# The last 96 columns of gate and up with rows on partitions, turned by a DMA transpose

## The chip, the cores and the metric

The kernel runs on one core of a Trainium2 chip. Its engines are TensorE (PE, which multiplies matrices and whose weight loads the profile lists as PEld), VectorE (DVE), ScalarE (ACT), GpSimd (POOL) and SyncE (SP, which issues DMA transfers). The metric is the device time of one execution in microseconds, as the median of several runs.

## What is computed

One transformer block on 2048 rows of 512 columns, in bf16. The first half is attention with 32 heads of 16 columns over a window of 8 rows, two apart; the second is a gated feed-forward layer of width F = 1376. `_ln` is the layernorm without weights:

```
h  = x + attention(_ln(x) @ wqkv) @ wo
n  = _ln(h)
gate = n @ W_gate                  # 512 x 1376
up   = n @ W_up                    # 512 x 1376
out  = h + (relu(gate) * up) @ W_down   # 1376 x 512
```

The feed-forward width is 1376 = 10 x 128 + 96. The 96 columns left over, the tail, are what the change is about.

## The kernel before

The rows are cut into four chunks of 512 (`tk` 0 to 3). For each chunk the kernel makes the layernorm, turns the result so that the 512 columns stand on partitions (four blocks `dt` of 128), forms q, k and v, makes the attention, projects with wo (L831) and adds the residual, makes the second layernorm into `hnT` (again columns on partitions, 128 x 4 x 512), and runs the feed-forward layer.

Gate and up are formed with the feature on partitions. For each block `ft` of 128 features, four matmuls (one per `dt`) have 128 x 128 of the weights as the stationary operand and 512 rows of `hnT` as the moving one (L869); one group of four makes up, one makes gate, each in a PSUM bank of its own. ACT copies up out of its bank (L873) and takes the relu of gate out of the other (L876); DVE multiplies two blocks at a time (L897) into `gT`, which has features on partitions and so can be the stationary operand of the down matmuls (L914) as it is. The eleventh block is the tail: the same 8 matmuls of 512 columns, but with 96 weight columns, and evictions and a product of 96 x 512. The down matmuls make, for each 128 rows, 11 matmuls of 512 columns into a bank; they come as a first part of blocks 0 to 7 and a second part of blocks 8 to 10, the tail among these. DVE adds the residual (L925) and a DMA stores the rows. In the last chunk the last 128 rows are done in two halves of 256 columns.

All of this is written as a list of steps, each with an engine, a planned duration, what it depends on and which buffers it takes. A planner (`Plan.order`) turns the list into one order for each engine. The rank of every step stands in a table of numbers, `RANK`, and on each engine steps go by rank, so that steps of different chunks are interleaved: gate and up of one chunk run on PE while DVE is still busy with the next chunk's attention. The engines carry out their streams strictly in this order. Buffers are taken from small sets: eight PSUM banks for everything, two each for `up_sb` and `gr`, seven for `gT`, five for rows of 128 x 512 (`row`, which serves normalised rows, squares and output rows).

Transfers: SP issues the loads at the start, the broadcasts of the attention weights (`big<-ex`, L730), the stores, and ten DMA transposes of normalised rows (L505) in its own order, one after the other; POOL issues the transfers that add halves of the attention products (L805). The other normalised rows are turned on PE by matmuls with the identity (L516).

Of the kernel before, what the change touches and what calls it, by code (L numbers as in the profile page):

```python
# [8 lines left out]
P = 128  # L9
BF16 = mybir.dt.bfloat16  # L10
# [81 lines left out]
class Plan:  # L92
# [9 lines left out]
    def add(self, key, *a, **k):  # L102
        op = Op(*a, **k)
        op.key = key
        op.seq = len(self.ops)
        if RANK:
            op.prio = RANK[op.seq]
        self.ops.append(op)
        for b in set(op.take) | set(op.use):
            b.left += 1  # L110
        return op
# [97 lines left out]
def kernel(  # L209
# [63 lines left out]
    wg_sb = sb.tile([P, NT, F], BF16, name="wg_sb")  # L273
    wu_sb = sb.tile([P, NT, F], BF16, name="wu_sb")
# [31 lines left out]
    def setup():  # L306
# [27 lines left out]
        nc.sync.dma_start(wu_sb[:], B_W_up.rearrange("(dt p) f -> p dt f", p=P))  # L334
        nc.sync.dma_start(wg_sb[:], B_W_gate.rearrange("(dt p) f -> p dt f", p=P))
# [45 lines left out]
    HSP = ()  # L381

# [157 lines left out]
    for tk in range(NCK):  # L540
# [317 lines left out]
        for f0 in range(0, NFT, 2):  # L858
            fts = range(f0, min(f0 + 2, NFT))
            ub, gr, gt = Buf(up_s), Buf(gr_s), Buf(gT_s)  # L860
            eds = []
            for ft in fts:
# [4 lines left out]
                def f_mm(w_sb, mm, lo=0, hi=CS, ft=ft, fs=fs, hnT=hnT):  # L867
                    for dt in range(NT):
                        nc.tensor.matmul(mm.t[:fs, lo:hi], lhsT=w_sb[:, dt, ft * P: ft * P + fs],  # L869
                                         rhs=hnT.t[:, dt, lo:hi], start=(dt == 0), stop=(dt == NT - 1))  # L870
# [7 lines left out]
                def mm(w_sb, b, wl, pr=pr, f0=f0, ft=ft, f=f_mm, hnT=hnT):  # L878
                    if (tk, ft) not in HSP:
                        return add(("mm%d" % (f0 // 2), tk), "PE", 4 * MM, lambda: f(w_sb, b), hev + [wload[wl]], pr,  # L880
                                   take=[b], use=[hnT], lat=PEL)
                    a = None
                    for i, (lo, hi, evs) in enumerate(((0, 2 * P, hev[0:1]), (2 * P, CS, hev[1:]))):
                        a = add(("mm%d%s" % (f0 // 2, "ac"[i]), tk), "PE", 2 * MM + 0.005, lambda lo=lo, hi=hi: f(w_sb, b, lo, hi),
                                evs + [wload[wl], a], pr, take=[b], use=[hnT], lat=PEL if i else 0.0)
                    return a

                a = mm(wu_sb, um, "u")
                b = add(("ue%d" % (f0 // 2), tk), "ACT", A5, f_ue, [a], pr - 200, take=[ub], use=[um], lat=AL)
                c = mm(wg_sb, gm, "g")  # L890
# [14 lines left out]
        if tk == NCK - 1:  # L905
            parts[-1:] = [(BPC - 1, 0, D // 2), (BPC - 1, D // 2, D)]
# [77 lines left out]
```

## Time and profile before

| | |
|---|---|
| median of 3 runs | 199.99 us (199.97 to 200.69) |
| the profiled execution | 201.04 us |
| its span, from the first to the last instruction | 199.3 us |
| PE busy | 193.6 us, 1099 matmuls |
| DVE busy | 153.2 us |
| ACT busy | 114.2 us |
| tail matmuls (128x96 weights, 512 columns) | 32 records of 379 ns |
| first to last matmul of the feed-forward layer | 66.93 to about 196.1 us |

An engine's busy time is the sum of the time in which it had an instruction in work. Matmuls are pipelined: one record of 512 columns has 379 ns, but the next begins about 216 ns after it, so their records overlap. In the lines below, "x16" is the number of instructions, "128x512" the partitions and elements of the tile written, and a bracket or the last column tells for how long the engine sat idle before and what ended that time.

### The profile page before, as it was taken

The page shows a single profiled execution, that of the slowest core. Times are in us where ns is not written, and L with a number is a line of the kernel's source. Part 1 is how long each engine was busy: PE and PEld are TensorE (multiplying, and loading weights), DVE is VectorE, ACT ScalarE, POOL GpSimd, SP SyncE. Part 2 cuts the span into 40 slices and gives each one's busy share as a digit, 9 for nine tenths or more (in the row PEclk, how much of TensorE's full clock was granted, in tenths as well). Part 3 has the DMA queues.
Part 4 walks back from the last instruction along what each step waited for, and adds up shares of the span by engine and source line. Part 5 has one row for each costly group of instructions (what it writes and reads, how often), then busy time and mean ns, then how long its engine had stood idle before and what let it go on. Part 6 is the DMA issues. An engine that isn't in the chain of part 4 may idle for free.

```text
span 199.3 us, 2971 instructions
## 1 busy us (share of the span) xinstructions
PE 193.6 (97%) x1099; PEld 96.2 (48%) x1099; DVE 153.2 (77%) x247; ACT 114.2 (57%) x234; POOL 12.7 (6%) x28
## 2 busy tenths in 40 slices
PE   8898999999999999999999999999999999999993
PEld 8755445655345444444444444444444444444452
DVE  6679999999999989999898899999982231024342
ACT  3447799966898766872726559513486455414500
POOL 4000000330000003200033000000000000000000
PEclk9999999999999999999999999999999999999999
DMA  5969970695000726953669971310013200000312
GB/s 161 336 218 346 405 233 2 129 188 104 3 0 0 163 51 128 189 104 83 157 117 187 181 209 50 73 32 0 3 53 81 53 0 0 3 0 0 132 53 79
DMA packets 18957, 21.44 MB, mean 108 GB/s; under 512 B 6560, under 2 KB 15744, under 8 KB 18944
## 3 DMA queue, kind: packets, MB, share of 16 engines
q1 hardware_dynamic: 16496, 14.13, 24.0%
q0 software_dynamic: 1728, 6.29, 16.9%
q10 hardware_dynamic: 720, 0.85, 1.3%
q8 instruction: 8, 0.13, 0.3%
q14 instruction: 5, 0.04, 0.1%
HBM read 8.42 MB, written 2.10 MB: 53 GB/s over the span
## 4 chain that ended last, share of the span: by engine, by line
PE 84%; DMA 7%; DVE 5%; ACT 2%; issue 0%; POOL 0%; DVEq 0%
PE bank L869 38%; PE bank L914 19%; PE bank L557 12%; DMA x_sm<-in_A_x_dram 7%; PE bank L831 7%; PE bank L612 3%; DVE big L606 2%; PE bank L516 2%; DVE big L765 1%; PE bank L690 1%; ACT kT L565 1%; DVE quad L769 1%; ACT quad L532 1%; PE bank L834 0%; DVE st L452 0%
## 5 line engine op out<-in xcount | busy, mean ns | idle before, releaser
L869 PE MATMUL bank<-quad,wu_sb 128*128 128x512 bf16 (+1 forms) x176 | 43.1, 379 | 0.0
L869 PE MATMUL bank<-quad,wg_sb 128*128 128x512 bf16 (+1 forms) x176 | 42.9, 379 | 0.1
L914 PE MATMUL bank<-wd_sb,gT 128*128 128x512 bf16 (+3 forms) x187 | 41.0, 367 | 0.0
L876 ACT ACTIVATE gr<-bank 128x512 bf16<-128x512 f32 (+1 forms) x44 | 25.2, 600 | 26.0 <-PE bank L869 21.6
L897 DVE TENSOR_TENSOR gT<-gr,up_sb 128x1024 bf16<-128x1024 bf16 (+1 forms) x24 | 15.1, 643 | 28.5 <-ACT up_sb L873 16.0
L873 ACT CAST up_sb<-bank 128x512 bf16<-128x512 f32 (+1 forms) x44 | 25.0, 589 | 16.1 <-PE bank L869 14.7
L557 PE MATMUL bank<-quad,wqk_sb 128*128 128x512 bf16 (+1 forms) x136 | 30.6, 367 | 0.3 <-ACT quad L532 0.2
L762 DVE TENSOR_TENSOR big<-big,vT 128x4096 bf16<-128x4096 bf16 x12 | 27.1, 2288 | 0.9 <-DMA big<-ex 0.7
L914 PEld LDWEIGHTS <-gT 128*128 128x128 bf16 (+1 forms) x187 | 18.1, 98 | 19.9 <-issue 0.4
L869 PEld LDWEIGHTS <-wg_sb 128*128 128x128 bf16 (+1 forms) x176 | 17.5, 100 | 20.9 <-issue 0.8
L606 DVE TENSOR_TENSOR big<-quad,kT 128x4096 bf16<-128x4096 bf16 x12 | 27.2, 2287 | 0.4 <-ACT kT L565 0.4
L869 PEld LDWEIGHTS <-wu_sb 128*128 128x128 bf16 (+1 forms) x176 | 17.5, 100 | 20.6 <-DMA big<-ex 0.4
L557 PEld LDWEIGHTS <-wqk_sb 128*128 128x128 bf16 x136 | 15.0, 114 | 13.0 <-issue 1.0
L765 DVE TENSOR_TENSOR big<-big 128x1024 bf16<-128x1024 bf16 (+2 forms) x24 | 16.8, 730 | 0.1
L805 POOL DMA_DIRECT2D big<-big x12 | 10.5, 875 | 87.7 <-DVE big L762 57.6
L557 PE MATMUL bank<-quad,wv_sb 128*128 128x512 bf16 x64 | 15.7, 380 | 0.0
L925 DVE TENSOR_TENSOR row<-x_sm,bank 128x512 bf16<-128x512 bf16 (+1 forms) x17 | 10.7, 652 | 5.9 <-PE bank L914 4.1
L831 PE MATMUL bank<-wo_sb,quad 128*128 128x512 bf16 x64 | 15.0, 379 | 0.3 <-DVE quad L769 0.3
L441 ACT ACTIVATE row<-x_sm,mv 128x512 bf16<-128x512 bf16 x12 | 8.6, 719 | 9.3 <-DVE mv L433 9.1
L532 ACT COPY quad<-bank 128x1024 bf16<-128x1024 bf16 (+1 forms) x11 | 10.3, 949 | 5.3 <-PE bank L516 5.3
L487 DVE TENSOR_SCALAR row<-x_sm,mv,rs 128x512 bf16<-128x512 bf16 x32 | 11.4, 407 | 1.7 <-ACT rs L469 1.7
L452 DVE BATCH_NORM_STATS2 st<-x_sm 128x6 f32<-128x512 bf16 x16 | 10.5, 676 | 2.7 <-DMA x_sm<-in_A_x_dram 2.7
(70 smaller groups left out, 159.1 us busy)
## 6 DMA issues: line engine op xcount, KB each, us to landing
big<-big POOLq DMA_DIRECT2D x12, 512.0 KB, 5.0
big<-ex SPq DMA_DIRECT2D x24, 128.0 KB, 3.0
out_dram<-row SPq DMA_DIRECT2D x15, 128.0 KB, 1.8
x_sm<-in_A_x_dram SPq DMA_DIRECT2D x3, 512.0 KB, 5.2
wu_sb<-in_B_W_up_dram SPq DMA_DIRECT2D x1, 1376.0 KB, 8.8
wg_sb<-in_B_W_gate_dram SPq DMA_DIRECT2D x1, 1376.0 KB, 11.8
wd_sb<-in_B_W_down_dram SPq DMA_DIRECT2D x1, 1280.0 KB, 15.1
wqk_sb<-in_A_wqkv_dram SPq DMA_DIRECT2D x2, 256.0 KB, 6.8
```

Of the source, the lines that this page charges most:

```text
L487: V.tensor_scalar(out=xn.t[:], in0=x, scalar1=mv.t[:, j, 0:1], scalar2=rs.t[:, j:j + 1], op0=ALU.add if residual else ALU.subtract, op1=AL ...
L532: nc.scalar.copy(out=o, in_=i)
L557: nc.tensor.matmul(mm.t[:, lo:hi], lhsT=wv_sb[:, dt, t:D:NT] if c == 2 else wqk_sb[:, dt, c * D + t:(c + 1) * D:NT], rhs=xnT.t[:, dt, lo:h ...
L606: V.tensor_tensor(out=pb.t[:].rearrange("p (t w) s -> p t w s", t=2), in0=q4, in1=k4, op=ALU.mult)
L762: V.tensor_tensor(out=mt.t[:], in0=ab.t[:], in1=v8, op=ALU.mult)
L765: V.tensor_tensor(out=mt.t[:, 0:n, :], in0=mt.t[:, 0:n, :], in1=mt.t[:, n:2 * n, :], op=ALU.add)
L831: nc.tensor.matmul(od.t[:], lhsT=OT.t[:, t, j * P:(j + 1) * P], rhs=wo_sb[:, t, :], start=(t == 0), stop=(t == NT - 1 and tk not in RPE))
L869: nc.tensor.matmul(mm.t[:fs, lo:hi], lhsT=w_sb[:, dt, ft * P: ft * P + fs], rhs=hnT.t[:, dt, lo:hi], start=(dt == 0), stop=(dt == NT - 1))
L873: nc.scalar.copy(out=ub.t[:fs, i, :], in_=um.t[:fs, :])
L876: nc.scalar.activation(out=gr.t[:fs, i, :], in_=gm.t[:fs, :], func=ACT.Relu)
L897: V.tensor_tensor(out=gt.t[:fs, 0:n, :], in0=gr.t[:fs, 0:n, :], in1=ub.t[:fs, 0:n, :], op=ALU.mult)
L914: nc.tensor.matmul(od.t[:, c0:c1], lhsT=gts[ft].t[:fs, ft % 2, j * P:(j + 1) * P], rhs=wd_sb[:fs, ft, c0:c1], start=(ft == 0), stop=(ft == ...
```

## The change

The tail leaves the scheme of the other blocks. For each 128 rows of the chunk, the 128 x 128 block of `hnT` is now the stationary operand and the moving one is the 96 gate columns and the 96 up columns together, 192 in all; the result has rows on partitions. That is 4 blocks of rows x 4 blocks `dt` = 16 matmuls of 192 columns for each chunk, in two banks (two blocks of rows each). To make the two strips one operand, the weights of gate and up lie in one tile, `wgu_sb`. For each bank ACT takes the relu of the gate strips into `gr`, and DVE multiplies them with the up strips straight out of PSUM into a `row` buffer. One DMA transpose on SP then turns the 128 x 512 row buffer into `gT`, where the down matmuls find the tail in the form they had before. The other ten blocks are formed as before; they are paired as before, and the tail had no partner before either.

All steps are ranked anew, in a new `RANK` table of 737 numbers in place of 729.

```
-    wg_sb = sb.tile([P, NT, F], BF16, name="wg_sb")
-    wu_sb = sb.tile([P, NT, F], BF16, name="wu_sb")
+    wgu_sb = sb.tile([P, NT, 2, F], BF16, name="wgu_sb")
...
-        nc.sync.dma_start(wu_sb[:], B_W_up.rearrange("(dt p) f -> p dt f", p=P))
-        nc.sync.dma_start(wg_sb[:], B_W_gate.rearrange("(dt p) f -> p dt f", p=P))
+        nc.sync.dma_start(wgu_sb[:, :, 1, :], B_W_up.rearrange("(dt p) f -> p dt f", p=P))
+        nc.sync.dma_start(wgu_sb[:, :, 0, :], B_W_gate.rearrange("(dt p) f -> p dt f", p=P))
...
+    TMT = (0, 1, 2, 3)
+    TTM, DTG, ATE = 0.0845, 0.35, 0.3
...
+            if tk in TMT and fts[-1] == NFF:
+                gt, ht, gr = Buf(gT_s), Buf(xn_s), Buf(gr_s)
+                gus = []
+                for b in range(2):
+                    bk = Buf(mm_s)
+                    def f_tt(b=b, bk=bk, hnT=hnT):
+                        for i in range(2):
+                            for dt in range(NT):
+                                nc.tensor.matmul(bk.t[:, 2 * i * FTAIL:2 * (i + 1) * FTAIL].rearrange("p (g f) -> p g f", g=2),
+                                                 lhsT=hnT.t[:, dt, (2 * b + i) * P:(2 * b + i + 1) * P],
+                                                 rhs=wgu_sb[:, dt, :, NFF * P:F], start=(i + dt == 0), stop=(i == 1 and dt == NT - 1))
+                    def f_te(b=b, bk=bk, gr=gr):
+                        y = bk.t[:, 0:4 * FTAIL].rearrange("p (j g f) -> p j g f", j=2, g=2)
+                        nc.scalar.activation(out=gr.t[:, b, 0:2 * FTAIL].rearrange("p (j f) -> p j f", j=2), in_=y[:, :, 0, :], func=ACT.Relu)
+                    def f_tg(b=b, bk=bk, ht=ht, gr=gr):
+                        y = bk.t[:, 0:4 * FTAIL].rearrange("p (j g f) -> p j g f", j=2, g=2)
+                        V.tensor_tensor(out=ht.t[:].rearrange("p (j c) -> p j c", j=BPC)[:, 2 * b:2 * b + 2, 0:FTAIL],
+                                        in0=gr.t[:, b, 0:2 * FTAIL].rearrange("p (j f) -> p j f", j=2), in1=y[:, :, 1, :], op=ALU.mult)
+                    a = add(("mm%d" % (f0 // 2), tk), "PE", 8 * TTM, f_tt, hev + [wload["u"], wload["g"]], mb + f0 * 0.1,
+                            take=[bk], use=[hnT], lat=PEL)
+                    a = add(("ge%d" % (f0 // 2), tk), "ACT", ATE, f_te, [a], mb + f0 * 0.1 - 200, take=[gr], use=[bk], lat=AL)
+                    gus.append(add(("gu%d" % (f0 // 2), tk), "DVE", DTG, f_tg, [a], mb + f0 * 0.1 - 200, take=[ht], use=[bk, gr], lat=DL))
+                def f_gtd(gt=gt, ht=ht):
+                    nc.sync.dma_start_transpose(out=gt.t[:, 0, :].rearrange("p (j c) -> p j c", j=BPC), in_=ht.t[:])
+                gds[NFF] = add(("gtd", tk), "SP", TDD, f_gtd, gus, mb + f0 * 0.1 - 200, take=[gt], use=[ht], lat=0.5, dq=(0.1, 0.64))
+                gts[NFF] = gt
+                continue
...
-                        nc.tensor.matmul(mm.t[:fs, lo:hi], lhsT=w_sb[:, dt, ft * P: ft * P + fs],
+                        nc.tensor.matmul(mm.t[:fs, lo:hi], lhsT=wgu_sb[:, dt, g, ft * P: ft * P + fs],
```

More of the change, by code (lines that the diff above doesn't have):

```diff
@@ L381 @@
     HSP = ()
+    TMT = (0, 1, 2, 3)
+    TTM, DTG, ATE = 0.0845, 0.35, 0.3
+    LASTC = (D // 2,)
     LNA = ((0, 0, 0, 0), (0, 0, 0, 0))
@@ L865, with f_mm @@
                 pr = mb + ft * 0.1
-                def f_mm(w_sb, mm, lo=0, hi=CS, ft=ft, fs=fs, hnT=hnT):
+                def f_mm(g, mm, lo=0, hi=CS, ft=ft, fs=fs, hnT=hnT):
                     for dt in range(NT):
-                        nc.tensor.matmul(mm.t[:fs, lo:hi], lhsT=w_sb[:, dt, ft * P: ft * P + fs],
+                        nc.tensor.matmul(mm.t[:fs, lo:hi], lhsT=wgu_sb[:, dt, g, ft * P: ft * P + fs],
                                          rhs=hnT.t[:, dt, lo:hi], start=(dt == 0), stop=(dt == NT - 1))
@@ L876, in f_ge, with mm @@
                     nc.scalar.activation(out=gr.t[:fs, i, :], in_=gm.t[:fs, :], func=ACT.Relu)
-                def mm(w_sb, b, wl, pr=pr, f0=f0, ft=ft, f=f_mm, hnT=hnT):
+                def mm(g, b, wl, pr=pr, f0=f0, ft=ft, f=f_mm, hnT=hnT):
                     if (tk, ft) not in HSP:
-                        return add(("mm%d" % (f0 // 2), tk), "PE", 4 * MM, lambda: f(w_sb, b), hev + [wload[wl]], pr,
+                        return add(("mm%d" % (f0 // 2), tk), "PE", 4 * MM, lambda: f(g, b), hev + [wload[wl]], pr,
                                    take=[b], use=[hnT], lat=PEL)
@@ L883, in mm @@
                     for i, (lo, hi, evs) in enumerate(((0, 2 * P, hev[0:1]), (2 * P, CS, hev[1:]))):
-                        a = add(("mm%d%s" % (f0 // 2, "ac"[i]), tk), "PE", 2 * MM + 0.005, lambda lo=lo, hi=hi: f(w_sb, b, lo, hi),
+                        a = add(("mm%d%s" % (f0 // 2, "ac"[i]), tk), "PE", 2 * MM + 0.005, lambda lo=lo, hi=hi: f(g, b, lo, hi),
                                 evs + [wload[wl], a], pr, take=[b], use=[hnT], lat=PEL if i else 0.0)
                     return a
-                a = mm(wu_sb, um, "u")
+                a = mm(1, um, "u")
                 b = add(("ue%d" % (f0 // 2), tk), "ACT", A5, f_ue, [a], pr - 200, take=[ub], use=[um], lat=AL)
-                c = mm(wg_sb, gm, "g")
+                c = mm(0, gm, "g")
                 d = add(("ge%d" % (f0 // 2), tk), "ACT", A5, f_ge, [c], pr - 200, take=[gr], use=[gm], lat=AL)
@@ L905 @@
         if tk == NCK - 1:
-            parts[-1:] = [(BPC - 1, 0, D // 2), (BPC - 1, D // 2, D)]
+            cs = (0,) + LASTC + (D,)
+            parts[-1:] = [(BPC - 1, a, b) for a, b in zip(cs, cs[1:])]
         for n, (j, c0, c1) in enumerate(parts):
```

72 rows, old and new, of the table RANK are left out of this document.

## The prediction

> **What bounds the kernel now.** I read the page's shares first, then busy time by stage, then TensorE's (PE's) timeline for pitches, then the forms of instructions for prices. From the page, first the busy times, then the chain that ended last:
>
> ```profile
> PE 193.6 (97%) x1099; PEld 96.2 (48%) x1099; DVE 153.2 (77%) x247; ACT 114.2 (57%) x234; POOL 12.7 (6%) x28
> ...
> PE 84%; DMA 7%; DVE 5%; ACT 2%; issue 0%; POOL 0%; DVEq 0%
> ```
>
> PE is busy nearly always and holds 84% of the chain. But matmuls overlap in the records, so I cut the span where each chunk's projection by wo begins (L831), to see where PE really had no gap. Columns: the stretch, its length, then busy time and count for PE, PEld, DVE, ACT, POOL:
>
> ```profile
> 9.80:52.00 42.20, 41.35 (x266) 21.57 (x265) 40.05 (x69) 32.45 (x63) 3.78 (x5) 1.00 0.67 193
> 52.00:90.20 38.20, 38.07 (x232) 17.60 (x233) 37.46 (x37) 28.40 (x61) 3.45 (x4) 1.00 0.42 83
> 90.20:117.30 27.10, 27.10 (x144) 12.28 (x143) 24.95 (x41) 14.07 (x29) 3.45 (x4) 1.00 0.75 155
> 117.30:142.70 25.40, 25.40 (x119) 11.78 (x118) 24.89 (x39) 12.05 (x27) 0.00 (x0) 1.00 0.20 48
> 142.70:196.10 53.40, 53.37 (x258) 25.35 (x256) 18.56 (x39) 22.95 (x46) 0.00 (x0) 1.00 0.13 38
> ```
>
> From 90.2 us on PE has no gap: every nanosecond taken from its stream comes off the end. Up to 90.2 DVE is as full as PE (40.05 of 42.20, 37.46 of 38.20), and there PE time is worth something only if DVE keeps up. The clock is 1.00 throughout. PE's timeline gives starts, from which I take the pitch, because a record's length contains the pipeline:
>
> ```profile
> 17.58 0.38 PE L557 MATMUL bank<-quad,wqk_sb 128*128 128x256 bf16 x2
> 17.80 0.39 PE L516 MATMUL bank<-identity,row 128*128 128x128 bf16 x4
> ...
> 35.82 1.06 PE L516 MATMUL bank<-identity,row 128*128 128x128 bf16 x16
> 36.71 1.03 PE L557 MATMUL bank<-quad,wv_sb 128*128 128x512 bf16 x4
> ...
> 52.01 1.04 PE L831 MATMUL bank<-wo_sb,quad 128*128 128x512 bf16 x4 [0.34 <-DVE quad L769]
> ...
> 125.89 7.07 PE L914 MATMUL bank<-wd_sb,gT 128*128 128x512 bf16 x32
> 132.80 1.03 PE L869 MATMUL bank<-quad,wg_sb 128*128 128x512 bf16 x4
> ```
>
> Start to start: 32 matmuls of 512 columns in 6.91 us, 0.216 each; two of 256 in 0.22, 0.110 each; 16 of 128 in 0.89, 0.0556 each. The first wo at 52.01 is the one place where PE visibly waits for DVE.
>
> **The change part by part.** *PE.* Per chunk it removes 8 matmuls of 512 columns (4 for up, 4 for gate; 96 of the 128 output rows used): 8 x 0.216 = 1.73 us. It adds 16 of 192 columns. Between 0.0556 at 128 and 0.110 at 256, 192 columns lie at 0.083, so 16 x 0.083 = 1.33 us. Over four chunks 6.91 becomes 5.31: 1.60 us less. Lower end 0.081 (192/512 of the 512 row): 1.73 less. Upper end 0.110 (as dear as 256, should two runs of 96 columns cost extra): 0.13 more. I take 0.083, since its neighbours on both sides lie on one line. The down matmuls stay 187.
>
> *Weight loads.* They double for the tail, 32 to 64, and are now of 128 columns. The rows to set against the pitch:
>
> ```profile
> L516 PEld LDWEIGHTS <-row 128*128 128x128 bf16 x88 | 5.8, 101 | 3.0 <-DVE row L487 1.6
> ...
> L869 PEld LDWEIGHTS <-wu_sb 128*96 128x96 bf16 x16 | 2.0, 123 | 1.6
> ```
>
> A record of about 100 ns would not fit under 83 ns, but the 16 transposes each have such a load and still start every 55.6 ns. So loads overlap and cost nothing here. The Trainium skill speaks against the change at this point: "TensorE: Matmul & The Clock Gate", section "LDWEIGHTS (loading the stationary operand)", gives columns/1.2 ns, 107 ns for 128 columns. If that set the pitch, the estimate would be 64 x 0.107 = 6.85 us, and PE would gain 0.06 us. The transposes' 55.6 ns do not bear that out.
>
> *ACT.* Removed per chunk: two evictions of 96x512 at 0.60. Added: two of 128x192, between 0.204 (128x4) and 0.600 (128x512): 0.35 each. 0.5 us less per chunk, off the path: ACT is 57% busy.
>
> *DVE.* Removed: one 96x512 product at 0.417. Added: two 128x192 products that read PSUM, priced by the output additions, which do the same:
>
> ```profile
> L925 DVE TENSOR_TENSOR row<-x_sm,bank 128x512 bf16<-128x512 bf16 x15 | 10.0, 682 | 5.1 <-PE bank L914 3.3 <-DMA out_dram<-row 1.8
> ...
> L897 DVE TENSOR_TENSOR gT<-gr,up_sb 96x512 bf16<-96x512 bf16 x4 | 1.7, 417 | 2.5 <-ACT up_sb L873 2.5
> ...
> L925 DVE TENSOR_TENSOR row<-x_sm,bank 128x256 bf16<-128x256 bf16 x2 | 0.8, 422 | 0.8 <-PE bank L914 0.8
> ```
>
> On the line through 422 and 682 a width of 192 is 0.36 us. So DVE gets 0.30 us more per chunk. Its cover is the distance to the next consumer, below.
>
> *SP and the transposes.* Four DMA transposes, each 1.22 us of issue on SP and 2.5 to landing, as the layernorm's:
>
> ```profile
> L505 SPq DMA_TRANSPOSE quad<-row x10: 1189/1216/1293, 97.7 to 153.5; - x10
> ...
> DMA to landing us min/median/max: 2.4/2.5/2.5
> ```
>
> Relu, product and transpose make 0.35 + 0.36 + 2.5 = 3.2 us from the last tail matmul to the first down matmul that reads it. In the changed order, PE work between the two, at the pitches above, is 11.3, 19.5, 15.4 and 22 us for the four chunks, so 8 us and more hide it. What is queued in between: in chunk 0 the transpose stands on SP behind the eight broadcasts of chunk 2 and ahead of two transposes of chunk 1's layernorm. Before, those broadcasts issued until 96.4 and the layernorm's transposes began at 97.67. Now the two DVE products that release the broadcasts stand earlier, so I put the new transpose at about 94 to 95 and its landing at 97; its reader is due at about 99. In chunk 1 the products stand on DVE behind three 2.29 us products of attention and hold two PSUM banks until about 131.6, by adding up the DVE rows from 120; PE writes these banks again at 133.6. In chunk 3 the transpose waits until about 179, behind an output addition, and its reader comes at about 189.
>
> *The one tile for both weights* moves no bytes, and both loads land well before the first use at 66.9: nothing.
>
> *The order.* The RANK table is new, so every engine's order changes. Summing PE work between the wo groups: to the first 45.5 us before and after; then 37.7 to 37.3, 26.9 to 26.1, 25.5 to 27.0, 53.2 to 51.3. The sums fall by the tail's saving alone. DVE's work ahead of the second wo grows by one 0.42 us product (0.34 start to start), the attention scaling of chunk 2, moved ahead. Before, DVE ended its last attention row at 89.8, PE came at 90.24 and reads that row 0.65 later: 1.1 us of slack, minus 0.34, minus 0.4 by which PE comes earlier, leaves 0.35. So it holds, barely. Ahead of the third wo DVE's sum is unchanged within 0.1, and PE arrives 1.3 earlier against rows that now have fewer waits (1.84 us of DVE's time there was idle): at par.
>
> In the first 52 us, where DVE paces, one wait goes:
>
> ```profile
> 15.31 0.69 DVE L452 BATCH_NORM_STATS2 st<-x_sm 128x6 f32<-128x512 bf16 x1 [0.65 <-DMA x_sm<-in_A_x_dram]
> ...
> 42.96 2.30 DVE L606 TENSOR_TENSOR big<-quad,kT 128x4096 bf16<-128x4096 bf16 x1 [0.42 <-ACT kT L565]
> ```
>
> Statistics that waited for chunk 2's rows now stand behind 2.4 us of products and normalisations that are ready. What is late next is the second line: ACT delivers kT at about 42.9 whatever DVE does, though one addition more is done before it now. I take 0.3 us off the first wo, with ends 0.65 off (all of the wait) and 0.5 on (another wait like the second line).
>
> **Sum.** The profiled execution took 201.04 us: a span of 199.3 and 1.7 around it. 201.04 - 1.60 - 0.3 = 199.1. It stood 1.05 above the median of 199.99, so on the median 199.99 - 1.9 = 198.1. Its own range adds the ends that I find plausible together: 197.4 (0.081 and 0.65) to 199.0 (0.083 to 0.09, and 0.2 lost early).
>
> **The rivals.** *Weight loads pace the tail.* If the 98 ns of a load's record were the pitch, 64 x 0.098 = 6.27, a gain of 0.64 and with the early 0.3 a time of 199.05. For it: the record. Against it: the transposes. If the pitch were the 0.110 of the upper end, 199.8.
>
> *DVE takes the gain.* Between 52 and 90 us DVE was busy 98%, and its waits (0.71 us for a broadcast at 72.5) are not in my sum. If the early saving fails (0.3) and DVE holds the second or third wo by 0.7 to 1.5 us, the time is 199.1 to 199.9. For it: a slack of only 0.35. Against it: the extra work there is one product.
>
> *Slower: the SP queue in chunk 1.* If the broadcasts ahead of the new transpose end late, it and the two layernorm transposes behind it come late, each 1.22 us of issue, and PE stands first at the second half of down (about 99) and then at chunk 1's first gate and up (about 101.5). There is 2 us of slack; every us beyond it is lost, and from 3.9 us late the change no longer pays. One broadcast's landing ranged from 2.5 to 6.7 us in this trace, so 5 us late is conceivable: 201.1. Against it: the median was 3.0, and DVE releases them earlier now.
>
> **How the numbers follow.** 0.5% (1.0 us) is about what these runs, 199.97 to 200.69, can tell from no change. The forecast has 0.72, weight loads 0.06, DVE taking the gain 0.11, SP 0.11. The predicted time is the forecast's, 198.1. Faster by over 0.5% means below 199.0: the forecast's 0.72 and a little of the second rival, 0.73. Within 0.5%: 0.16. Slower: 0.11. The range 197.0 to 200.2 takes in the first two rivals and leaves out the third.
>
> **What would show it.** In the changed profile: the tail's 16 matmuls starting every 0.083 us, with 0.098 or 0.110 for the first rival; no PE gap between the tail and the down matmuls behind it; wo groups starting at about 51.7, 89.5, 115.6, 142.7; the new transposes at 1.2 us of issue and 2.5 to landing; the page's 97% unchanged. A wait of PE on a transpose, or on DVE at the second or third wo, of more than 1 us would make the prediction wrong.

## The result, and the profile after

The changed kernel took 198.58 us (median of 4 runs, 198.14 to 198.79) against 200.11 us for the kernel before on the same chip (4 runs, 199.97 to 200.69): a ratio of 0.9916, with a 95% interval of 0.9888 to 0.9944. Measured twice more, it was at 0.9888 (0.9860 to 0.9915) and 0.9897 (0.9877 to 0.9917). It is about 1% faster; the three differences of the medians are 1.5, 2.4 and 1.9 us, and the forecast had 1.9. The two profiled executions lie further apart, 201.04 and 198.39 us, which is 2.65.

The page of the changed kernel, the same two lines as before: busy times, and the chain that ended last.

```profile
PE 190.5 (97%) x1111; PEld 97.1 (49%) x1131; DVE 154.0 (78%) x251; ACT 111.7 (57%) x234; POOL 12.7 (6%) x28
...
PE 66%; DMA 14%; issue 13%; DVE 4%; POOL 1%; SPq 1%; POOLq 0%; DVEq 0%
```

PE has 3.1 us less, DVE 0.8 more, ACT 2.5 less. Not all of the 3.1 us is saved work: this profile has 1111 records for 1131 matmuls (it has 1131 weight loads, one for each). The second profile of the changed kernel has all 1131 and 191.6 us, 2.0 less than before. PE's part of the chain went from 84% to 66%: the chain is now followed through DVE and a transfer, because PE waits for them at a new place, the third wo. (In the run below in which that wait is gone, PE holds 92%.) The wait shows in PE's timeline (start, length, line, form, count, idle time before):

```profile
50.95 1.03 PE L833 MATMUL bank<-wo_sb,quad 128*128 128x512 bf16 x4
...
85.56 1.48 PE L873 MATMUL bank<-wgu_sb,quad 128*128 128x192 bf16 x16
86.88 1.89 PE L952 MATMUL bank<-wd_sb,gT 128*128 128x512 bf16 x7
88.61 3.62 PE L833 MATMUL bank<-wo_sb,quad 128*128 128x512 bf16 x16
...
115.25 3.63 PE L833 MATMUL bank<-wo_sb,quad 128*128 128x512 bf16 x15 [0.33 <-DVE quad L801]
...
142.27 3.62 PE L833 MATMUL bank<-wo_sb,quad 128*128 128x512 bf16 x16
```

L833 is the projection by wo (L831 before). Its four starts were 52.01, 90.24, 117.26 and 142.74. The tail (L873) takes 1.32 us from its first start to the next line's, 0.0825 for each matmul, and the down matmuls (L952) follow without a gap. The second wo starts without a wait, the third with one of 0.33 us. That is the idle time behind the last record, and a record's length contains the pipeline. By starts the wait costs more: 44 matmuls of 512 columns stand ahead of it from 105.26 on, one every 0.216 us, so it could have started at 114.76 and started 0.49 later.

Two lines of the kernel before belong beside these. The first is a wait of PE for DVE in the first 52 us, the second the third wo, which had no wait:

```profile
16.70 1.04 PE L516 MATMUL bank<-identity,row 128*128 128x128 bf16 x12 [0.51 <-DVE row L487]
...
117.26 3.62 PE L831 MATMUL bank<-wo_sb,quad 128*128 128x512 bf16 x16
```

The new operations, by form (busy time and mean ns of one, then idle time before and what ended it):

```profile
L873 PE MATMUL bank<-wgu_sb,quad 128*128 128x192 bf16 x64 | 6.3, 246 | 0.0
L873 PEld LDWEIGHTS <-quad 128*128 128x128 bf16 x64 | 5.5, 98 | 1.4
...
L879 ACT ACTIVATE gr<-bank 128x192 bf16<-128x192 f32 x8 | 2.6, 339 | 1.2 <-DVE gT L934 1.1
L883 DVE TENSOR_TENSOR row<-gr,bank 128x192 bf16<-128x192 bf16 x8 | 2.5, 348 | 0.8 <-ACT gr L879 0.8
```

A matmul's record has 246 ns and a weight load's 98 ns, and yet matmuls start every 82.5 ns: the records overlap, and only the starts give the price.

**An account that closes.** Three sections of a profile explain its whole length: the start of DVE's first statistics that waited for rows from HBM (when those rows had landed); from there to the first wo; and from the first wo to DVE's last output addition. I use it for all runs below; all numbers are starts in the trace.

| kernel | rows there | to the first wo | first wo to last addition |
|---|---|---|---|
| before | 10.80 | 41.21 | 144.10 |
| before, second profile | 10.51 | 41.09 | 144.10 |
| changed | 10.87 | 40.08 | 142.80 |
| changed, second profile | 10.13 | 40.38 | 142.81 |
| changed, third profile | 9.91 | 40.49 | 143.50 |

From 201.04 to 198.39: the rows came 0.07 us later; the way to the first wo is 1.13 shorter; the rest is 1.30 shorter; what follows the last addition is 0.34 shorter (3.19 to 2.85), and what lies around the span 0.05 longer (1.74 to 1.79). 201.04 + 0.07 - 1.13 - 1.30 - 0.34 + 0.05 = 198.39.

PE's starts say what the two large pieces are. *Up to the first wo* the kernel before lost PE time to DVE twice: 0.67 us ahead of the transposes at 16.70 (two matmuls of 512 columns that began at 15.60 take 0.43), and 0.41 ahead of the first wo at 52.01. Together that is 1.08 of the 1.13. The changed kernel has neither wait: from the first matmul with wv, at 12.22, to the first wo PE never waits. In the nine profiles with the new order that leave the statistics where they are, this stretch takes 38.70 to 38.73 us, however early the rows landed. *From the first wo on* the tail gives 1.63 (6.91 less 64 x 0.0825 = 5.28). Another 0.19 comes from the change from small matmuls of attention (L612) to chunk 0's first gate and up, which took 0.50 from start to start before (66.43 to 66.93), where such a change takes 0.31 elsewhere. The new wait takes 0.49 back. 1.63 + 0.19 - 0.49 = 1.33, against 1.30 in the table.

### The profile page after: what moved, and what is told of

Same layout as the page of the kernel before. It is cut to its first block, busy times and chain, and to the rows that moved or that the text cites. A ratio compares the mean times of both kernels' runs of the same rounds, so it can differ in the third digit from the quotient of the medians.

```text
span 196.6 us, 3034 instructions
## 1 busy us (share of the span) xinstructions
PE 190.5 (97%) x1111; PEld 97.1 (49%) x1131; DVE 154.0 (78%) x251; ACT 111.7 (57%) x234; POOL 12.7 (6%) x28
## 4 chain that ended last, share of the span: by engine, by line
PE 66%; DMA 14%; issue 13%; DVE 4%; POOL 1%; SPq 1%; POOLq 0%; DVEq 0%
PE bank L906 20%; PE bank L559 19%; PE bank L952 14%; DMA big<-big 7%; PE bank L833 5%; DMA wv_sb<-in_A_wqkv_dram 4%; PE bank L614 2%; DVE big L764 2%; PE bank L873 2%; PE bank L518 2%; DMA x_sm<-in_A_x_dram 1%; POOL big L807 1%; DMA big<-ex 1%; DVE big L608 1%; PE bank L836 1%
## 5 line engine op out<-in xcount | busy, mean ns | idle before, releaser
L906 PE MATMUL bank<-quad,wgu_sb 128*128 128x512 bf16 x313 | 72.0, 379 | 0.4
L906 PEld LDWEIGHTS <-wgu_sb 128*128 128x128 bf16 x320 | 31.0, 98 | 37.3 <-issue 0.8
L952 PE MATMUL bank<-wd_sb,gT 128*128 128x512 bf16 (+2 forms) x182 | 40.1, 366 | 0.3
L913 ACT ACTIVATE gr<-bank 128x512 bf16<-128x512 f32 x40 | 23.2, 603 | 26.0 <-PE bank L906 24.5
L910 ACT CAST up_sb<-bank 128x512 bf16<-128x512 f32 x40 | 23.2, 594 | 16.5 <-PE bank L906 14.0
L934 DVE TENSOR_TENSOR gT<-gr,up_sb 128x1024 bf16<-128x1024 bf16 x20 | 13.7, 689 | 22.7 <-ACT up_sb L910 16.8
L952 PEld LDWEIGHTS <-gT 128*128 128x128 bf16 (+1 forms) x187 | 18.1, 98 | 19.5 <-issue 0.4
L833 PE MATMUL bank<-wo_sb,quad 128*128 128x512 bf16 x62 | 14.7, 379 | 0.4 <-DVE quad L801 0.3
L489 DVE TENSOR_SCALAR row<-x_sm,mv,rs 128x512 bf16<-128x512 bf16 x32 | 11.4, 407 | 1.8 <-ACT rs L471 1.8
L567 ACT CAST kT<-bank 128x512 bf16<-128x512 f32 x16 | 8.9, 598 | 5.7 <-PE bank L559 5.5
L567 ACT CAST quad<-bank 128x512 bf16<-128x512 f32 x16 | 9.5, 607 | 3.6 <-PE bank L559 3.6
```

The source lines that it names most:

```text
L567: nc.scalar.copy(out=o, in_=mm.t[:])
L833: nc.tensor.matmul(od.t[:], lhsT=OT.t[:, t, j * P:(j + 1) * P], rhs=wo_sb[:, t, :], start=(t == 0), stop=(t == NT - 1 and tk not in RPE))
L906: nc.tensor.matmul(mm.t[:fs, lo:hi], lhsT=wgu_sb[:, dt, g, ft * P: ft * P + fs], rhs=hnT.t[:, dt, lo:hi], start=(dt == 0), stop=(dt == NT ...
L910: nc.scalar.copy(out=ub.t[:fs, i, :], in_=um.t[:fs, :])
L913: nc.scalar.activation(out=gr.t[:fs, i, :], in_=gm.t[:fs, :], func=ACT.Relu)
L934: V.tensor_tensor(out=gt.t[:fs, 0:n, :], in0=gr.t[:fs, 0:n, :], in1=ub.t[:fs, 0:n, :], op=ALU.mult)
```

## The experiments

The theory was that the gain is the tail's 1.6 us of PE time plus an earlier first wo by the new order, and that the rest is hidden. The rivals: the weight loads pace the tail; DVE takes part of the gain; the transposes on SP cost time; all of it is the new order. The table holds all profiled runs in the columns above, with the wait of PE at the third wo, as recorded and by starts. The changed kernel's three profiles have 0.33, 0.34 and 0.74 there, and 0.49, 0.50 and 0.91 by starts.

| run | rows there | to the first wo | first wo to last addition | wait at the third wo | by starts |
|---|---|---|---|---|---|
| new tail, old order | 10.78 | 40.45 | 143.29 | none | none |
| old tail, new order | 10.53 | 40.19 | 144.39 | 0.29 | 0.45 |
| tail as 128 matmuls of 96 | 10.60 | 40.08 | 143.03 | 0.40 | 0.56 |
| each new transpose twice | 10.68 | 40.09 | 142.87 | 0.39 | 0.56 |
| each new product three times | 10.59 | 40.07 | 144.75 | 1.02 | 1.19 |
| statistics early | 10.75 | 40.61 | 142.79 | 0.32 | 0.48 |
| third wo later | 10.66 | 40.08 | 142.47 | none | none |
| third wo later, again | 10.56 | 40.08 | 142.46 | none | none |

### The new tail in the old order

The operations of the changed kernel, with the ranks of the kernel before; the new steps take the ranks of the old tail's steps. Only the table differs:

```
 RANK = [
...
-    25, 27, 32, 39, 18, 21, 23, 24, 26, 30, 40, 42, 29, 34, 36, 37, 41, 43, 46, 22,
+    22, 25, 33, 28, 18, 21, 23, 26, 27, 31, 36, 39, 30, 35, 38, 40, 42, 46, 49, 24,
...
```

> The changed kernel with the tail in its new form, but every other step at the rank it had in the kernel before; the tail's new steps take the ranks of the old tail's. Theory (the form of the tail makes the gain, 1.6 us of PE time): about 1.6 us below the kernel before, 198.5, less whatever PE loses to banks held longer by the product, which in the old order stands behind the residual sums of chunk 1 (up to 0.5 us). The first wo then starts as before, near 52. Rival (the new order makes the gain, the form is swallowed by waits): within 0.5 us of the kernel before, 199.6 to 200.6.

Measured: 199.19 us (198.91 to 199.63) against 200.36, ratio 0.9937 (0.9920 to 0.9955). The form alone gives 1.2 us, less than its theory had: 199.19 lies 0.2 above the 198.5 to 199.0 that it allowed. The first wo came at 51.23, and not near 52, because the rows of chunk 2 landed in time. From the first wo on, the trace is 0.81 shorter than before's 144.10, and not 1.63: PE has two new gaps. PE's timeline of this run:

```profile
149.82 0.81 PE L906 MATMUL bank<-quad,wgu_sb 128*128 128x512 bf16 x3
150.94 4.48 PE L906 MATMUL bank<-quad,wgu_sb 128*128 128x512 bf16 x20 [0.31 <-DVE row L883]
155.82 6.20 PE L906 MATMUL bank<-quad,wgu_sb 128*128 128x512 bf16 x28 [0.41 <-issue]
```

At 0.216 us for each matmul (one record is missing in the first line), PE lost 0.25 us ahead of 150.94 and 0.56 ahead of 155.82: 0.81, and 1.63 - 0.81 = 0.82, as the account has it. The first gap ends with the new product (L883), which holds the PSUM bank until DVE gets to it; for the second the profile names no releaser. So in the old place of DVE's stream the new product comes late for at least one bank. With the new order PE has neither gap.

### The old tail in the new order

```
-    TMT = (0, 1, 2, 3)
+    TMT = ()
```

With this, the old tail's code runs on the one weight tile, with the changed kernel's ranks for all other steps.

> The tail as before (8 matmuls of 512 columns, two evictions, one product), in the one weight tile, with all steps in the changed kernel's order. Theory (form): the PE sum is that of before, so 0 to 1 us below it, 199.1 to 200.1, the gain being the earlier first wo alone (51.0 in the changed kernel, 52.0 before). Rival (order): 1.2 to 1.6 us below the kernel before, like the changed kernel.

Measured: 200.01 us (199.66 to 200.33) against 200.36, ratio 0.9979 (0.9968 to 0.9990). The order alone gives 0.4 us, as the theory of the form had it. In the trace it is 0.9 to 1.0 us faster to the first wo, and then 0.29 us slower than before (144.39 against 144.10): by starts, 0.45 lost at the third wo less the 0.19 that the new order saves at the first gate and up. So the wait at the third wo belongs to the new order, with either tail. Against the changed kernel this run is 144.39 - 142.80 = 1.59 us longer: the tail's form, with everything else alike.

### Twice the weight loads

Each matmul of 192 is split into gate and up, 96 columns each, so that 128 matmuls each load their own 128 columns of weights.

```
-                                nc.tensor.matmul(bk.t[:, 2 * i * FTAIL:2 * (i + 1) * FTAIL].rearrange("p (g f) -> p g f", g=2),
-                                                 lhsT=hnT.t[:, dt, (2 * b + i) * P:(2 * b + i + 1) * P],
-                                                 rhs=wgu_sb[:, dt, :, NFF * P:F], start=(i + dt == 0), stop=(i == 1 and dt == NT - 1))
+                                for g in range(2):
+                                    nc.tensor.matmul(bk.t[:, (2 * i + g) * FTAIL:(2 * i + g + 1) * FTAIL],
+                                                     lhsT=hnT.t[:, dt, (2 * b + i) * P:(2 * b + i + 1) * P],
+                                                     rhs=wgu_sb[:, dt, g, NFF * P:F], start=(i + dt + g == 0), stop=(i + g == 2 and dt == NT - 1))
```

> Each tail matmul of 192 columns is split into two of 96 (gate strip, up strip): 128 matmuls and 128 weight loads instead of 64. It asks where the weight load begins to set the pitch. If columns alone set it (line through 0.0556 at 128 and 0.0825 at 192): 0.042 us each, 5.4 us in all, the changed kernel's time within 0.3 us. If a load of 128 columns cannot start more often than every 0.055 us: 7.0 us in all, 1.8 us above the changed kernel, so the gain would be gone. If each load takes the 0.098 us of its record: 12.5 us, 7 us above.

Measured: 198.38 us (198.22 to 199.71), ratio 0.9914 (0.9884 to 0.9943): the changed kernel's time. PE's timeline, with a half tail between other groups, and the weight loads by form:

```profile
120.28 0.84 PE L874 MATMUL bank<-wgu_sb,quad 128*128 128x96 bf16 x16
120.96 1.03 PE L907 MATMUL bank<-quad,wgu_sb 128*128 128x512 bf16 x4
```

```profile
L874 PEld LDWEIGHTS <-quad 128*128 128x128 bf16 x128 | 6.1, 98 | 1.4
```

Sixteen matmuls, each with its own load of 98 ns, take 0.68 us: 42.5 ns each. 128 x 0.0425 = 5.44 us against 64 x 0.0825 = 5.28 is 0.16 more, and the account shows it: 143.03 less the 0.56 that it lost at the third wo is 142.47, the changed kernel's 142.80 less 0.49 is 142.31. A load of 98 ns does not pace a stream even at 42.5 ns. The Trainium skill, "TensorE: Matmul & The Clock Gate", section "Back-to-back issue gap", gives N/2.4 + 2.5 ns as the gap of an isolated matmul of N columns at the full clock, and says that a stream with a weight load for every matmul is slower at small N, about 81 ns at N = 128. The trace agrees with the formula, by which one estimates 82.5 and 42.5 ns, in just such a stream (granted clock 0.998), and not with the slower figure: 128 columns started every 55.6 ns in the kernel before. Nor does it bear out the 107 ns of the same page's section "LDWEIGHTS (loading the stationary operand)" as a pace.

### The kernel before, once more

No edit: a second look at the kernel before, to see how much of its late first wo belongs to one execution.

> The kernel before once more, for a second profile. The profiled execution that the prediction was read from took 201.04 us against a median of 199.99, with the first wo at 52.01. If that start is the order's doing, it is at 52.0 again and the span near 199.3. If it was that execution's own delay, the first wo starts 0.5 to 1.1 us earlier and the span is about 198.3.

Measured: 200.65 us for this one execution. The two lines that matter are PE's first wo and, on DVE, the statistics of chunk 2's rows:

```profile
51.60 1.04 PE L831 MATMUL bank<-wo_sb,quad 128*128 128x512 bf16 x3 [0.34 <-DVE quad L769]
```

```profile
14.91 0.69 DVE L452 BATCH_NORM_STATS2 st<-x_sm 128x6 f32<-128x512 bf16 x1 [0.55 <-DMA x_sm<-in_A_x_dram]
```

The first wo came 0.41 us earlier than in the first profile, between what the two theories had. Of that, 0.29 is earlier rows (10.51 against 10.80). The way from there to the first wo is the same within 0.12, and the wait for chunk 2's rows is there again (0.55 against 0.65). So the start of a kernel varies with the landing of its first loads, and that has to be taken out ahead of any comparison of starts.

### Each new transpose twice

```
                     nc.sync.dma_start_transpose(out=gt.t[:, 0, :].rearrange("p (j c) -> p j c", j=BPC), in_=ht.t[:])
+                    nc.sync.dma_start_transpose(out=gt.t[:, 1, :].rearrange("p (j c) -> p j c", j=BPC), in_=ht.t[:])
```

The second copy goes to the unused half of the same `gT` buffer.

> The changed kernel with each of the four new DMA transposes issued twice (the second into the unused half of the same gT buffer, and the down matmuls wait for it too as far as the buffer is shared). Theory (the transposes are hidden: SP has a gap of 1.8 us behind the first, and 8 us or more of PE work lie before each reader): the changed kernel's time within 0.3 us, 198.3 to 198.9. Rival (SP's queue is on the path in chunk 1): the two layernorm transposes behind the first come 1.2 us later and PE waits for them, 0.5 to 1.2 us more.

Measured: 198.98 us (198.55 to 199.19), ratio 0.9916 (0.9895 to 0.9938). SP's timeline, the changed kernel first and then this run:

```profile
92.59 1.31 SPq L892 DMA_TRANSPOSE gT<-row  x1
95.70 2.50 SPq L507 DMA_TRANSPOSE quad<-row  x2
```

```profile
91.95 1.32 SPq L892 DMA_TRANSPOSE gT<-row  x1
93.33 1.25 SPq L893 DMA_TRANSPOSE gT<-row  x1
95.53 2.50 SPq L507 DMA_TRANSPOSE quad<-row  x2
```

The doubled transpose fits into the gap ahead of chunk 1's layernorm transposes, and these are not later. From the first wo to the last addition it is 142.87, the changed kernel's 142.80 and 0.07 more at the third wo. So even four transposes more hold up no engine, and the four of the change don't either. The median is another matter: 198.98 is just above the expected 198.3 to 198.9, and 0.8 above the 198.16 of the unedited kernel on the same chip. About 0.35 us of that lies outside the span: the time less the span is 2.09 to 2.19 us in all four executions, and 1.72 to 1.92 in all others. What takes it there, no run shows. The rest is within the scatter of the spans (196.4 to 197.0 here, 195.7 to 197.4 there).

### Each new product three times

```
+                        for _ in range(3):
-                        V.tensor_tensor(out=ht.t[:].rearrange("p (j c) -> p j c", j=BPC)[:, 2 * b:2 * b + 2, 0:FTAIL],
-                                        in0=gr.t[:, b, 0:2 * FTAIL].rearrange("p (j f) -> p j f", j=2), in1=y[:, :, 1, :], op=ALU.mult)
+                            V.tensor_tensor(out=ht.t[:].rearrange("p (j c) -> p j c", j=BPC)[:, 2 * b:2 * b + 2, 0:FTAIL],
+                                            in0=gr.t[:, b, 0:2 * FTAIL].rearrange("p (j f) -> p j f", j=2), in1=y[:, :, 1, :], op=ALU.mult)
```

> The changed kernel with each of the eight new DVE products carried out three times, 1.1 us more DVE work per chunk. Theory (DVE paces PE up to the third wo, where PE already waited 0.3 to 0.5 us for it; later work is covered): the products of chunk 0 stand ahead of the third wo, so 0.8 to 1.2 us more than the changed kernel, seen as a longer gap ahead of the third wo; chunks 1 to 3 cost at most 0.3 us. Rival (DVE has cover everywhere): within 0.3 us of the changed kernel. Second rival (every product is on the path): 4 us more.

Measured: 199.07 us (198.77 to 200.05), ratio 0.9932 (0.9905 to 0.9959). That is 0.9 us above the 198.16 of the unedited kernel on the same chip, within the 0.8 to 1.2 that was expected. The profiled execution, 200.05, was the slowest of the four, and its trace is 1.95 us longer from the first wo on (144.75 against 142.80). DVE's timeline, the changed kernel first, then this run, and last the changed kernel's third profile:

```profile
88.94 0.61 DVE L883 TENSOR_TENSOR row<-gr,bank 128x192 bf16<-128x192 bf16 x2
...
114.04 0.69 DVE L767 TENSOR_TENSOR big<-big 128x1024 bf16<-128x1024 bf16 x1 [1.16 <-DMA big<-big]
114.77 0.42 DVE L801 TENSOR_TENSOR quad<-big 128x512 bf16<-128x512 bf16 x1
```

```profile
71.24 6.70 DVE L764 TENSOR_TENSOR big<-big,vT 128x4096 bf16<-128x4096 bf16 x3 [1.03 <-DMA big<-ex]
...
89.69 2.17 DVE L884 TENSOR_TENSOR row<-gr,bank 128x192 bf16<-128x192 bf16 x6
...
115.67 0.69 DVE L767 TENSOR_TENSOR big<-big 128x1024 bf16<-128x1024 bf16 x1 [1.86 <-DMA big<-big]
```

```profile
71.11 6.69 DVE L764 TENSOR_TENSOR big<-big,vT 128x4096 bf16<-128x4096 bf16 x3 [1.15 <-DMA big<-ex]
```

This is how the third wo comes to wait. The products of chunk 0's tail (0.61 us for the two) stand on DVE ahead of the four long attention products that POOL's transfers wait for. POOL's last transfer of the four is issued at 105.74 in the changed kernel and 107.44 here; it lands some 8 us later (DVE's wait for it ends at 114.04 and 115.67), DVE makes the last attention row (L801), and PE's third wo reads that.

Why the trace is longer by 1.95: 1.03 us of DVE's lateness is this run's first line, a broadcast that landed late, 15 us ahead of any repeated product. The changed kernel's third profile has the same late broadcast (1.15 us) with no edit at all, and takes 143.50 from the first wo on. So a late broadcast by itself costs some 0.7 us (143.50 against 142.80), and the four added products ahead of the third wo some 1.25 (144.75 against 143.50). PE's starts show where: against the changed kernel it loses 0.70 more at the third wo, 0.64 and 0.41 at 97.75 and 98.39, where its own transposes wait for normalised rows, and 0.14 within the second wo, 1.89 in all. Behind the third wo the twelve other repetitions cost nothing: from its start to the last output addition it is 78.50 us in the changed kernel (115.25 to 193.75) and 78.53 here (116.88 to 195.41).

### The third wo later

If the wait is PE's being early, and not DVE's being slower, then two groups of gate and up (8 matmuls, 1.73 us) put ahead of the third wo should remove it.

```
-    514, 519, 523, 522, 527, 524, 535, 508, 533, 504, 536, 539, 513, 532, 544, 517, 530, 547, 549, 541,
+    514, 519, 523, 522, 527, 524, 535, 494, 533, 492, 536, 539, 513, 532, 544, 517, 530, 547, 549, 541,
...
-    456, 479, 420, 428, 454, 467, 433, 441, 471, 477, 499, 507, 492, 496, 497, 502, 494, 498, 510, 512,
+    456, 479, 420, 428, 454, 467, 433, 441, 471, 477, 508, 507, 497, 496, 504, 502, 499, 498, 510, 512,
```

> The changed kernel with the third wo (chunk 2) two gate-and-up groups (1.73 us of PE work) later in PE's order. Theory (PE loses 0.3 to 0.5 us there waiting for DVE's last attention row): that gap closes and the time falls by 0.3 to 0.5 us, 198.1 to 198.3, since the layernorm behind it had about 3 us of slack. Rival (what is gained there is lost where chunk 2's gate and up begin, or in the banks): no change, or 0.5 us more.

> The changed kernel once more, on the chip of these runs, as their measure. Expected 1.4 to 1.9 us below the kernel before; the first wo starts between 50.6 and 51.0, whatever the loads do, where in the kernel before it ranged from 51.6 to 52.0.

Measured beside each other: 197.84 us (197.56 to 197.85), ratio 0.9859 (0.9839 to 0.9879), and for the changed kernel without an edit 198.16 (197.53 to 199.20). The unedited kernel's first wo came at 50.51, a little ahead of the expected 50.6 to 51.0, so it is not independent of the loads. A second pair gave the same sign:

> The variant with the third wo two groups later, once more beside the changed kernel. Theory: 0.3 to 0.4 us below the changed kernel of this call, as PE's stream from the first wo to its last matmul was 0.35 us shorter in the traces. Rival (chance): no difference of the medians, or the other sign.

> The changed kernel as the measure for this call: 1.5 to 2.4 us below the kernel before.

197.79 us (197.65 to 198.28), ratio 0.9880 (0.9860 to 0.9899), against 198.41 (197.81 to 198.74). The medians are 0.3 and 0.6 us apart, the intervals overlap. The traces are clear. PE's timeline of the edited kernel and DVE's:

```profile
105.06 11.39 PE L906 MATMUL bank<-quad,wgu_sb 128*128 128x512 bf16 x52
116.28 3.62 PE L833 MATMUL bank<-wo_sb,quad 128*128 128x512 bf16 x16
```

```profile
117.34 0.69 DVE L844 SCALAR_TENSOR_TENSOR x_sm<-x_sm,bank 128x512 bf16<-128x512 bf16 x1 [1.08 <-PE bank L833]
```

PE runs into the third wo with no gap, and now DVE waits for PE, 1.08 us, which is what has room there. From the first wo to the last addition it takes 142.47 and 142.46 us, 0.33 less than the changed kernel. By starts that is the 0.49 of the third wo less 0.15 that PE now loses within the fourth, whose line is 3.78 us long in place of 3.62:

```profile
141.56 3.78 PE L833 MATMUL bank<-wo_sb,quad 128*128 128x512 bf16 x16
```

This is the best of the kernels that were run, 1.2 to 1.4% faster than the kernel before.

### The statistics back in their old place

The forecast had put the earlier first wo down to the statistics of chunk 2's rows, which before stood behind the first attention product and waited there. This run puts the two steps of these statistics that had moved back near that place, by rank alone:

```
-    466, 411, 424, 448, 485, 67, 73, 59, 65, 52, 64, 57, 63, 75, 76, 83, 88, 79, 86, 93,
+    466, 411, 424, 448, 485, 67, 70, 59, 65, 52, 64, 57, 63, 76, 77, 84, 88, 80, 87, 93,
...
-    582, 647, 681, 543, 607, 616, 678, 531, 614, 624, 649, 537, 634, 638, 724, 87, 104, 124, 144, 129,
+    582, 647, 681, 543, 607, 616, 678, 531, 614, 624, 649, 537, 634, 638, 724, 72, 104, 124, 144, 129,
```

The ranks between 70 and 87 move by one or two to make room.

> The changed kernel with one step of the order put back: the first statistics of chunk 2's rows (0.6 us on DVE) stand behind the first product of attention, as in the kernel before, and not behind the second product and the normalisations. Theory (this step makes the early start hang on when the rows of chunk 2 land): DVE waits at it by as much as the load is late, 0 to 0.7 us, and the first wo comes later than the 50.5 to 51.0 of the changed kernel by what it waited; the time rises by the same, up to 0.7 us. Rival (the early gain lies in other steps): DVE waits there, but the first wo stays at 50.5 to 51.0.

Measured: 198.69 us (198.30 to 198.94), ratio 0.9914 (0.9895 to 0.9933). Neither theory had it: DVE did not wait there, and still the first wo came late. DVE's timeline of this run:

```profile
14.68 0.69 DVE L454 BATCH_NORM_STATS2 st<-x_sm 128x6 f32<-128x512 bf16 x1
15.28 1.21 DVE L623 TENSOR_TENSOR big<-quad,kT 128x2048 bf16<-128x2048 bf16 x1
16.41 1.37 DVE L489 TENSOR_SCALAR row<-x_sm,mv,rs 128x512 bf16<-128x512 bf16 x4
```

The same stretch of the changed kernel:

```profile
14.67 1.19 DVE L623 TENSOR_TENSOR big<-quad,kT 128x2048 bf16<-128x2048 bf16 x1
15.78 1.38 DVE L489 TENSOR_SCALAR row<-x_sm,mv,rs 128x512 bf16<-128x512 bf16 x4
17.08 1.27 DVE L454 BATCH_NORM_STATS2 st<-x_sm 128x6 f32<-128x512 bf16 x2
```

Counted from the landing of the rows, the normalised rows of L489 begin at 5.66 us here and at 4.91 in the changed kernel, 0.75 later, and the first wo comes 0.53 later (40.61 against 40.08). PE's timeline shows what lies between, the changed kernel first and then this run:

```profile
16.99 1.06 PE L518 MATMUL bank<-identity,row 128*128 128x128 bf16 x16
17.89 3.62 PE L559 MATMUL bank<-quad,wv_sb 128*128 128x512 bf16 x15
```

```profile
16.88 0.39 PE L518 MATMUL bank<-identity,row 128*128 128x128 bf16 x4
17.52 0.94 PE L518 MATMUL bank<-identity,row 128*128 128x128 bf16 x12 [0.25 <-DVE row L489]
18.30 3.62 PE L559 MATMUL bank<-quad,wv_sb 128*128 128x512 bf16 x15
```

The sixteen transposes take 0.90 us in the changed kernel and 1.42 here, because PE waits for the later rows: 0.52 us. From there to the first wo both need 33.06 us. ACT follows PE: a copy of kT begins at 42.48 here and 42.08 there. So the statistics cost half a microsecond without any wait at them, through the normalised rows that stand behind them.

This isn't the cost that the old order had. In this run the second product of attention stands ahead of the rows too (L623 at 15.28), which it didn't before. In the first run, with the old order and rows that landed in time, the rows of L489 began at 15.16, and PE began the transposes at 15.94 with no wait; what was left there was the wait of 0.41 at the first wo, and with it DVE's wait for kT (0.42, at 42.19). That wait for kT is gone in the changed kernel, where DVE starts that product at 41.94. The likely reason is that ACT there makes four copies of kT in one row from 39.69, where before the reciprocal (L696) stood between the second and the third; no run takes this step alone.

## Why the prediction was right, and where its steps were not

The time, 198.1, is 0.1 to 0.5 us below the three measured medians (198.16, 198.41, 198.58); the direction was right, and the main term was right to 0.03 us. Two smaller terms were wrong, with opposite signs, and that they partly cancel is luck. (The lower end of the forecast's own range was added up wrongly: 199.99 - 1.73 - 0.65 is 197.6 and not 197.4.)

- **The tail, 6.91 to 5.31 us, -1.60.** 5.28 was measured, -1.63; the pitch was forecast at 0.083 and is 0.0825. With all else alike the tail's form is worth 1.59 us.
- **Weight loads cost nothing.** Right, and with more room than the forecast's row showed: they still hide at 42.5 ns. The rival of the loads pacing the tail is refuted.
- **ACT and DVE, 0.35 and 0.36 us.** Records of 0.339 and 0.348.
- **The transposes are hidden; SP stays ahead.** Right: 1.19 to 1.31 us of issue, 2.4 to 2.7 to landing, chunk 0's at 92.59 in place of the expected 94 to 95, chunk 3's at 182.0 in place of 179, and no wait of PE on any. The rival that SP's queue makes the kernel slower is refuted by the doubled transposes, which hold up nothing within the span.
- **One tile for both weights, nothing.** The old tail on that tile shows nothing beside the wait that the order brings.
- **The first wo, -0.3, with 0.65 as the far end.** Mis-sized. The way from the landed rows to the first wo is 1.0 to 1.1 us shorter. Two steps failed. "The first wo at 52.01 is the one place where PE visibly waits for DVE" was a misreading: PE also waited at 16.70, for the rows that stood behind the late statistics (0.51 as recorded, 0.67 by starts), so DVE's wait of 0.65 was PE's too and came off whole. And "ACT delivers kT at about 42.9 whatever DVE does" was wrong: ACT's copies depend, through PE, on these rows, and in the run with the old order, where the rows came in time, DVE's wait for kT came at 42.19 in place of 42.96. In the changed kernel this second wait is gone as well, and with it the 0.41 at the first wo; which of the moved steps did that, no run separates.
- **The second wo, slack of 0.35, "holds, barely".** Held: 37.66 us after the first, forecast 37.8, no wait.
- **The third wo, "at par".** Wrong: PE waits 0.33 us, 0.49 by starts. In the other profiles of the changed order, apart from the edits made to this wait, it is 0.29 to 0.40 (0.45 to 0.56 by starts), and 0.74 (0.91) where a broadcast landed late. The forecast compared DVE's sum, which is unchanged, with PE's arrival, and took 1.84 us of DVE's idle time as a reserve. It isn't one: DVE's last row waits for POOL's transfer (1.16 us), which was released by products some 8 us earlier, so idle time of DVE behind those products cannot be used. This is a small part of the second rival (DVE takes the gain).
- **"97% unchanged", and no PE gap of over 1 us at the second or third wo.** Both as forecast.

On traces, the forecast's -1.9 was really -1.63 - 1.1 - 0.19 + 0.49 = -2.4. The 0.19, at chunk 0's first gate and up, was not in the forecast. The medians' differences were 1.5, 2.4 and 1.9 us, so they can't tell -1.9 from -2.4. How early a run's first loads land adds to that scatter: 9.91 to 10.87 us in five profiles of the two kernels.

## What to carry to other kernels

For an operand with fewer than 128 columns left over, swapping the stationary and the moving operand makes the matmuls pay only for columns that are used, provided that something off the critical path can turn the result back. The price of the new form is to be read from starts of neighbouring forms, not from the length of a record or of a weight load; the same goes for a wait, whose idle time behind a record is too short (0.33 for 0.49 here). A wait on one in-order engine can come out as a wait of the next: look through that engine's whole timeline for it before a later wait is said to hide it. And when PE comes earlier, look at what releases the row it reads. If that is a transfer issued long before, the engine's idle time behind the issue is no reserve; other matmuls that are ready can be moved ahead of the reader.

## What the runs showed of the hardware

- A matmul of 96 columns with its own load of 128 weight columns starts every 42.5 ns, while the load's record has 98 ns: loads overlap each other and the matmuls by more than a factor of two.
- The landing of the first row loads moved by up to 0.96 us between profiles (9.91 to 10.87 us), and the first wo with it by up to 0.55 in one and the same kernel (50.40 to 50.95). When the rows came earliest, at 10.13 and 9.91, the way to the first wo was 0.3 to 0.4 longer: there PE's own stream set it, 38.70 us from the first matmul with wv (11.81 and 11.70) to the first wo.
- A broadcast on SP's queue that lands late by about 1.1 us shows in two of ten profiles with the new order, both times at the same DVE instruction (at about 71 us). In the one of them that had no edit the third wo, 44 us behind it, came 0.69 us later, counted from the first wo. The kernel before had a wait of 0.71 at that instruction in its first profile.
